# A gated attention and a token mixer in one kernel: the opening planned like the body, transfers handed over later, keys and queries turned as one

## The chip, the cores and the metric

The kernel runs on one core of a Trainium2 chip. The core has a matrix engine (TensorE, PE in the profile), three elementwise engines (VectorE or DVE, ScalarE or ACT, GpSimd or POOL) and SyncE (SP), whose queue only issues transfers here. All transfers run on sixteen DMA engines; some of them turn (transpose) a tile of two-byte numbers on the way. The metric is the device time of one execution in microseconds, lower is better. The kernel before takes 846.6 us, the median of three runs (846.22, 846.6 and 854.43).

## What is computed

```python
# batch 8, seq 3200, d_model 256, d_qk = d_hyper = 64
scores = (1/S) * z @ z.T                  # per batch, 3200 x 3200, symmetric
attn   = maximum(scores, 0) ** 2
x      = u * (attn @ v)                   # 3200 x 256
wq, wk = x @ w_q, x @ w_k                 # 3200 x 64
W_tok  = (1/8) * wq @ wk.T                # 3200 x 3200, no activation
mixed  = W_tok @ x
out    = maximum(mixed, 0) @ w_out        # float32
```

## The kernel before

**Tiles.** The 3200 rows of a batch are 25 tiles of 128. They are also seven groups of columns: six of 512 (four tiles) and one of 128. For each group the kernel goes over all 25 tiles. A score pair (line 220) makes two tiles of `scores` against the group, 128 x 512 each, into one of two PSUM slots. A first stage (lines 239 and 243, ACT or DVE) takes the positive part to SBUF as float32, which empties the slot; a second stage (line 256 on ACT, line 258 on POOL) squares it to fp16 in a buffer `at`, of which there are 14. The second product (line 299) multiplies `at` by v into four accumulator banks, two halves of a group by two half-arrays. Scores are symmetric, so a block of tiles that a group makes for one of the next two groups, or for the last, is not computed again: a DMA transpose (line 278) turns it from `at` into `tt` or `ttl`. Such blocks are called turned tiles.

**After a group.** ACT and DVE add the banks (lines 315 and 316), POOL multiplies by u (line 320) and the result x is turned by DMA (line 345) to `xT`. Projections of x give queries and keys together (line 362), ACT writes them out as fp16 `qk` (line 375). Keys are turned by DMA (line 382), two transposes of 64 rows by 256 columns for each full group, and doubled by POOL (line 394); "heads" (line 401) sum keys times x over all rows, 64 x 256 numbers, since the mixer has no activation between its two products. When a batch is through, "mix" (line 429) and the last product (line 452) make its outputs, beside the next batch's groups. The last groups of the last batch have a sequence of their own from line 946 on.

**z.** The score product wants z turned and standing twice, one copy in each half of the partitions. For batch 0 z is loaded in four chunks as float32, cast twice (line 118), turned on TensorE (line 127) and copied from PSUM (line 130). For later batches POOL's queue loads z as fp16 (line 141), DVE copies it twice in a row (line 146), and five DMA transposes turn it (line 152).

**Order of work.** Every engine and every issuing queue does its instructions in the order written. That order is written by a planner in the kernel's Python (lines 512 to 898): it keeps a clock for each of PE, DVE, ACT and POOL, books a weight for each step, and picks the next step of TensorE by these clocks. A transfer for SP is a `move(ready, due, issue, takes, fn, landed)`: it may be handed over when the PE clock passes `ready`, the one with the earliest `due` goes first, SP is booked for `issue`, and the DMA for `takes`; `landed` then tells the planner when the data can be used. So a transfer that stands early in SP's order, but whose data comes late on the chip, holds up all behind it. POOL's queue also issues loads (v and the later z), between its squares. The weights in the planner are the kernel's own numbers, not measurements.

**Opening.** The first eight score pairs, the first eight tiles of the second product, the chunks of z and the loads of v of batch 0 are written out by hand (lines 816 to 842), with tiles in the order 0 to 24; the planner takes over behind them, with made-up ready times for what the opening has begun. v comes in five loads, which stand in POOL's queue between casts and squares. The weights' seven transfers are issued in one go (line 171).

Of the kernel before, what the change touches and what calls it, by code (L numbers as in the profile page):

```python
# [16 lines left out]
def kernel(  # L17
# [74 lines left out]

    ZCH = [(0, 4), (4, 6), (10, 7), (17, 8)]
    ident = consts.tile([P, P], FP16, tag="ident", name="ident")
# [13 lines left out]

    def cast_first(c):
        n0, nn = ZCH[c]  # L110
        casts = [
            (nc.vector.tensor_copy, nc.scalar.copy),
            (nc.scalar.copy, nc.gpsimd.tensor_copy),
            (nc.gpsimd.tensor_copy, nc.vector.tensor_copy),
            (nc.gpsimd.tensor_copy, nc.vector.tensor_copy),
        ][c]
        for half, cast in enumerate(casts):
            cast(out=zd0[:, n0 : n0 + nn, half, :], in_=z32[n0][:])

    def turn_first(c):  # L120
        n0, nn = ZCH[c]
        if c < 2:
            tp = acc_tile(1, c, "ztp", FP16)
        else:
            tp = pps.tile([P, 4 * W], FP16, tag="ps", name="ztp")
        for i in range(nn):
            nc.tensor.transpose(
                tp[:, ts(i, P)], zd0[:, n0 + i, :, :].rearrange("p a k -> p (a k)"), ident
            )
        nc.vector.tensor_copy(out=zT[0][:, ds(n0 * P, nn * P)], in_=tp[:, 0 : nn * P])  # L130

# [10 lines left out]

    def double_z(b):
        zds[b] = pz.tile([P, NT, 2, dqk], FP16, tag="zd", name="zd")
        for half in range(2):
            nc.vector.tensor_copy(out=zds[b][:, :, half, :], in_=zdense[b][:])

# [23 lines left out]
    def load_weights():  # L171
        wo32[0] = px.tile([P, ND, D], FP32, tag="x_sb", name="wo32")
        for r in range(2):
            for w32, w in ((wq32, moe_w_q), (wk32, moe_w_k)):
                nc.sync.dma_start(out=w32[top(r), :, :], in_=w.rearrange("(c p) h -> p c h", p=dh))
        for half in range(2):
            nc.sync.dma_start(
                out=wk2[:, :, half, :], in_=moe_w_k.rearrange("(c p) h -> p c h", p=P)
            )
        nc.sync.dma_start(out=wo32[0][:], in_=moe_w_out.rearrange("(c p) e -> p c e", p=P))  # L180

# [15 lines left out]
    for b in range(B):  # L197
        for gi in range(NG):
            near = [t for t in range(NT) if is_turned(gi, group_of(t))]
            own = [  # L200
                t for t in range(NT) if t not in near and not is_turned(group_of(t), gi)
            ]
            if b == 0 and gi == 0:
                order = sorted(near + own)
            elif len(tiles) % 2:
                order = own[:1] + near + own[1:]
            else:
                order = near + own
            tiles += [(b, gi, t) for t in order]
            ends[b, gi] = len(tiles)  # L210
# [4 lines left out]
    def scores(p):  # L215
        assert len(ztimes) >= 5 * tiles[2 * p + 1][0]
        sc = ps_tile("sc")
# [159 lines left out]
    def turn_keys(b, gi):  # L377
        nn = widths[gi] // P
        ks[b, gi] = pk.tile([P, 4, 2, dh], FP16, tag="kx", name="kx")
        for r in halves(gi):  # L380
            n = min(2, nn - 2 * r)
            nc.sync.dma_start_transpose(
                out=ks[b, gi][:, 2 * r : 2 * r + n, 1 - r, :],
                in_=qks[b, gi][top(1 - r), r, 0 : n * P],
            )

# [135 lines left out]
    pending, later, extras, keyed, kept = [], [], [], [], []  # L522
    keys_at, out_of, turned_at = {}, {}, {}
    produced, stored = [0], []
# [3 lines left out]
    sp_at, dma_at = [0.0], [0.0]  # L528
    LANDS = 4.0

    def at_time(t, fn):
# [36 lines left out]
    def close_slot(t):  # L568
        slots.append(t)

    def use_pair():
        open_slot()
        p = produced[0]
        produced[0] += 1
        sc = scores(p)
        clock[PE] += 0.22
        ready = clock[PE] + FROM_PE
# [6 lines left out]
    def squares():  # L584
        while pending and pending[0][0] <= clock[PE] + 0.3:
# [25 lines left out]
    def use_keys(b, gi):  # L611
# [7 lines left out]
        if prior:  # L619
# [52 lines left out]
    def use_proj(b, gi):  # L672
# [12 lines left out]

        move(done + 0.2, done + 6.0, 0.55, 1.6, stores[0], landed)

# [4 lines left out]
    def batch_begun(b, t):  # L692
        if b + 1 < B:
            t += 10 if b == 0 else 0
            at_time(t + 6, lambda: (load_z(b + 1), push(3.0)))
            at_time(t + 20, lambda: double_z(b + 1))
            for i in range(5):
                move(t + 24 + 6 * i, t + 40 + 6 * i, 1.5, 1.0, lambda i=i: turn_z(b + 1, i))
            for i in range(5):
                at_time(t + 20 + 13 * i, lambda i=i: (load_v(b + 1, 5 * i, 5), push(2.5)))  # L700

    def group_begun(b, gi, t):
        if gi == 0:
            batch_begun(b, t)
        if gi + 1 < NG:
            move(t + 2, t + 6, 0.55, 1.6, lambda: load_u(b, gi + 1))
        elif b + 1 < B:
            move(t + 2, t + 6, 0.55, 1.6, lambda: load_u(b + 1, 0))

    SPARE = 0.5  # L710
    BIAS = 0.2
    GUARD = 12
    LATE = 0.3

    def half_done(b, gi, half):
# [21 lines left out]
    def open_rows():  # L737
# [6 lines left out]
        b, gi, left, fresh = (current[x] for x in ("b", "gi", "left", "fresh"))  # L744
        ready = [t for t in left if row_at.get((b, gi, t), 1e9) <= clock[PE]]
        mine = [t for t in ready if (b, gi, t) in made]
# [33 lines left out]
    def acc_step():  # L780
# [6 lines left out]
        fn()  # L787
        clock[PE] += 0.1093
        used.add(row)
# [4 lines left out]
    def calm(weight):  # L794
# [5 lines left out]
        return max(first, clock[PE] + 0.5) + weight <= shut + LATE  # L800

    def all_used(p):
        return all(x in used for x in tiles[2 * p : 2 * p + 2])

    accumulate = lambda rows_, first=False: [
        fn()
        for half in range(2)
        for ti in rows_
        for fn in second_product(0, 0, half, ti, first and ti == rows_[0], False)
    ]  # L810

    def first_pair(p, on_act):
        for _, turn in second_stage(p, first_stage(p, scores(p), on_act), on_act):
            turn()

# [9 lines left out]
    first_pair(1, False)  # L825
    cast_first(2)
    first_pair(2, True)
    load_first_v(4, 6)
    accumulate([0, 1], first=True)
    turn_first(2)  # L830
    first_pair(3, False)
    accumulate([2, 3])
    first_pair(4, True)
    cast_first(3)
    load_first_v(10, 8)
    first_pair(5, False)
    accumulate([4, 5])
    turn_first(3)
    first_pair(6, True)
    accumulate([6, 7])  # L840
    first_pair(7, False)
    load_first_v(18, 7)
    produced[0] = 8
    groups.pop(0)
    current.update(b=0, gi=0, left=list(range(8, NT)), fresh=False)
    for p in range(8):
        for x in tiles[2 * p : 2 * p + 2]:
            b, gi, ti = x
            row_at[x] = 0.4 * p - 1.0
            if ti < 8:  # L850
                used.add(x)
            if is_turned(gi, group_of(ti)):
                for n in range(4):
                    row_at[b, group_of(ti), n] = 14.0
    at_time(3.0, lambda: load_u(0, 0))
    at_time(9.0, load_weights)
    at_time(20.0, cast_weights)
    group_begun(0, 0, 0.0)

    total = B * sum(NT * (w // P) for w in widths)  # L860
    done_acc = 32
    lead = 140
    turn_about = False
    while groups or work or current["left"]:
# [15 lines left out]
        p = produced[0]  # L880
        able = p < NPAIR and (p < NAT or all_used(p - NAT) and turned_at.get(p - NAT, 0.0) <= now and not out_of.get(p - NAT))
        wanted = able and p * total < (done_acc + lead) * NPAIR
# [131 lines left out]
```

## Time and profile before

| What | us |
|---|---|
| median of three runs | 846.6 |
| the profiled execution, its own time | 841.71 |
| its span, first to last instruction | 839.9 |
| TensorE busy | 780.0 (93%) |
| POOL busy | 613.7 (73%) |
| ACT busy | 577.6 (69%) |
| DVE busy | 479.1 (57%) |

The profile is of one execution, and its rows have times from the start of the span. A row of a group gives line, engine and operation, output and inputs, shapes, count, busy time, mean time of one in ns, and the idle time just before with what ended it. A row of the timeline begins with its start and its length. A matmul's length in a row holds its way through the array, and one starts before the last ends; so the rate is read from many in a row. DMA queue q1 holds what SP issues, q0 what POOL issues.

### The profile page before, as it was taken

The numbers are of one execution on the slowest core, as the hardware profiler recorded it, in microseconds if no ns is written. First come the engines' busy times: TensorE is split into PE (matmuls) and PEld (weight loads), VectorE is DVE, ScalarE is ACT, GpSimd is POOL, SyncE is SP. The second block draws the span as 40 slices with busy tenths as digits, with TensorE's granted clock in tenths as the row PEclk, the third lists the DMA queues.
The fourth block names the chain that finished last, engine by engine and source line by source line (L and its number), as shares of the span: only waits on it lengthen the run. The fifth ranks groups of instructions, "written<-read, shape, count | busy, mean of one in ns | idle before, by whom it ended". The sixth has DMA issues, their size and how long they took to land. (4 is left out here: it accounts for less than half of the span.)

```text
span 839.9 us, 28273 instructions
## 1 busy us (share of the span) xinstructions
PE 780.0 (93%) x12373; PEld 651.2 (78%) x12373; DVE 479.1 (57%) x501; ACT 577.6 (69%) x672; POOL 613.7 (73%) x513
## 2 busy tenths in 40 slices
PE   5799899999989998889989999999999999999995
PEld 3689788887778887768878877878778878878783
DVE  3576456654576536546558645655546654575533
ACT  4677677775767766756766766777677675877735
POOL 4797577877778657949968666978598886886750
PEclk9999999999999999999999999999999999999999
DMA  5999999999989988999597998999989999888725
GB/s 108 171 189 151 150 164 156 142 193 198 175 155 153 171 192 172 114 225 195 118 166 144 149 207 175 156 155 197 175 177 174 151 197 198 141 149 170 159 59 197
DMA packets 299101, 138.36 MB, mean 165 GB/s; under 512 B 276832, under 2 KB 279776, under 8 KB 298976
## 3 DMA queue, kind: packets, MB, share of 16 engines
q1 hardware_dynamic: 292064, 120.37, 77.5%
q0 software_dynamic: 6768, 15.98, 14.0%
q8 instruction: 97, 1.59, 0.8%
q14 instruction: 28, 0.23, 0.1%
q10 hardware_dynamic: 144, 0.20, 0.1%
HBM read 59.64 MB, written 26.21 MB: 102 GB/s over the span
## 5 line engine op out<-in xcount | busy, mean ns | idle before, releaser
L299 PE MATMUL acc<-v_sb,at 64*128 64x256 f16 x7312 | 500.5, 271 | 9.8 <-DMA v_sb<-in_v_dram 5.0
L258 POOL TENSOR_TENSOR at<-g 128x1024 f16<-128x1024 f32 (+2 forms) x236 | 426.6, 1823 | 80.3 <-DVE g L243 62.6
L299 PEld LDWEIGHTS <-at 64*128 64x128 f16 x7312 | 387.3, 95 | 79.2 <-issue 19.6
L243 DVE TENSOR_SCALAR g<-sc 128x1024 f32<-128x1024 f32 (+2 forms) x302 | 350.5, 1181 | 136.7 <-PE sc L220 123.5
L256 ACT ACTIVATE at<-g 128x1024 f16<-128x1024 f32 (+1 forms) x232 | 243.0, 1052 | 30.5 <-DVE g L243 26.6
L239 ACT ACTIVATE g<-sc 128x1024 f32<-128x1024 f32 x166 | 170.0, 1024 | 79.0 <-PE sc L220 77.9
L220 PE MATMUL sc<-zT 64*128 64x512 f16 x920 | 176.9, 380 | 13.1 <-DVE g L243 11.2
L320 POOL TENSOR_TENSOR x_sb<-both,u_sb 128x512 f16<-128x512 f32 (+1 forms) x112 | 133.0, 1195 | 71.6 <-DVE both L316 68.8
L299 PE MATMUL acc<-v_sb,tt 64*128 64x256 f16 x2304 | 164.1, 269 | 0.0
L316 DVE TENSOR_TENSOR both<-acc,both 128x512 f32<-128x512 f32 (+1 forms) x104 | 69.2, 670 | 129.1 <-ACT both L315 122.2
L299 PEld LDWEIGHTS <-tt 64*128 64x128 f16 x2304 | 121.6, 94 | 13.3
L315 ACT COPY both<-acc 128x512 f32<-128x512 f32 (+1 forms) x104 | 57.9, 563 | 39.7 <-PE acc L299 36.7
L220 PEld LDWEIGHTS <-zT 64*128 64x128 f16 x920 | 55.4, 94 | 28.3 <-issue 20.7
L375 ACT CAST qk<-qk 128x512 f16<-128x512 f32 (+1 forms) x54 | 29.4, 544 | 57.4 <-PE qk L401 52.2
L477 ACT ACTIVATE fo<-fo 128x1024 f32<-128x1024 f32 (+2 forms) x54 | 47.7, 890 | 29.7 <-PE fo L452 22.7
L442 ACT ACTIVATE rt<-mx 128x1024 f16<-128x1024 f32 (+1 forms) x56 | 52.2, 932 | 17.2 <-PE mx L429 17.1
L394 POOL COPY kx<-kx 128x128 f16<-128x128 f16 (+1 forms) x101 | 26.5, 289 | 48.4 <-DMA kx<-qk 48.3
L452 PE MATMUL fo<-wo,rt 128*128 128x256 f16 x400 | 52.8, 274 | 1.8 <-ACT rt L442 1.8
L416 DVE TENSOR_TENSOR ha<-qk,ha 128x512 f32<-128x512 f32 x37 | 25.6, 691 | 47.1 <-ACT qk L375 47.1
L362 PE MATMUL qk<-xT_sb,wqk 64*128 64x256 f16 (+1 forms) x404 | 32.9, 271 | 17.1 <-DMA xT_sb<-x_sb 17.0
L452 PEld LDWEIGHTS <-rt 128*128 128x128 f16 x400 | 35.0, 98 | 16.0 <-issue 10.1
L362 PEld LDWEIGHTS <-wqk 64*128 64x128 f16 x416 | 21.5, 95 | 23.2 <-DMA xT_sb<-x_sb 18.9
(42 smaller groups left out, 220.8 us busy)
## 6 DMA issues: line engine op xcount, KB each, us to landing
u_sb<-in_u_dram SPq DMA_DIRECT2D x48, 512.0 KB, 4.6
out_dram<-fo SPq DMA_DIRECT2D x40, 512.0 KB, 4.9
v_sb<-in_v_dram POOLq DMA_DIRECT2D x35, 320.0 KB, 6.5
out_dram<-fo SPq DMA_DIRECT2D x16, 256.0 KB, 2.0
zn<-in_z_dram POOLq DMA_DIRECT2D x7, 400.0 KB, 7.1
tt<-at SPq DMA_TRANSPOSE x144, 4.5
kx<-qk SPq DMA_TRANSPOSE x101, 3.7
u_sb<-in_u_dram SPq DMA_DIRECT2D x8, 128.0 KB, 3.8
```

Of the source, the lines that this page charges most:

```text
L220: nc.tensor.matmul(out=sc[:, h, 0:gw], lhsT=zT[b][top(h), ts(ti, P)], rhs=zT[b][top(h), ds(gs, gw)], start=True, stop=True,)
L239: nc.scalar.activation(out=g[:, hs, 0:w], in_=sc[:, hs, 0:w], func=RELU, scale=GSCALE)
L243: nc.vector.tensor_scalar(out=g[:, hs, 0:w], in0=sc[:, hs, 0:w], scalar1=0.0, scalar2=GSCALE, op0=AOP.max, op1=AOP.mult,)
L256: nc.scalar.square(out=out, in_=g[:, hs, 0:w])
L258: nc.gpsimd.tensor_mul(out=out, in0=g[:, hs, 0:w], in1=g[:, hs, 0:w])
L299: nc.tensor.matmul(out=accs[half, r][:, ds((j % 2) * D, D)], lhsT=weights(b, gi, ti, j)[top(r), :], rhs=vs[b][top(r), ti, :], start=(first ...
L315: nc.scalar.copy(out=both[:, 0 : n * D], in_=accs[half, 0][:, 0 : n * D])
L316: nc.vector.tensor_add(out=both[:, 0 : n * D], in0=accs[half, 1][:, 0 : n * D], in1=both[:, 0 : n * D])
L320: nc.gpsimd.tensor_mul(out=xs[b, gi][:, 0:n, :, r, :].rearrange("p n c d -> p (n c) d"), in0=both[:, 0 : n * D].rearrange("p (m d) -> p m ...
L362: nc.tensor.matmul(out=ps[:, r, 0 : n * P], lhsT=wqk[top(r), c, :, :].rearrange("p t h -> p (t h)"), rhs=xTs[b, gi][top(r), 0:n, c, :], st ...
L442: nc.scalar.activation(out=out, in_=ps[:, 0:nr, 0 : ND * n * P], func=RELU)
L452: nc.tensor.matmul(out=banks[r][:, ds(j * D, D)], lhsT=flat[:, ds((dc * n + j) * P, P)], rhs=wo[:, dc, :], start=(dc == 0 and j == 0), sto ...
```

## The change

The opening is left to the planner. Tiles of the first group are taken in another order: first those that are not to be turned (0 to 3 and 12 to 23), then 4 to 11 and 24. The chunks of z are loaded and turned in that order, all turns of z stand ahead of the first second product, and go through the four accumulator banks; the copy out of PSUM goes to ACT or DVE by their clocks. All five loads of v are issued on POOL's queue ahead of the first square. The planner's clocks start at times written by hand, PE's weights are doubled before 11 us, and v has times from which it may be used. The loads of u and of the weights become moves.

The planner's model of transfers is changed: SP is booked 1.28 us for each transpose, whatever its size, and 0.21 us of DMA for each 128 columns; SP is held when the DMA is more than 2 us behind (`RING`); a transfer may be handed over 1 us after its data is planned to be there (`SLACK`), not 0.2 or 0.3; x is due for turning 5 us after (`XDUE`), not 8; the projections are planned 3 us after x has landed (`XWAIT`). A load of u is handed over only when POOL's clock has passed.

The two copies of z on DVE are planned 3 us apart and booked with 0.98 us each. Keys and queries of a group are turned by one DMA transpose of 128 rows; the half that holds queries is overwritten by POOL's doubling copy.

```diff
-    ZCH = [(0, 4), (4, 6), (10, 7), (17, 8)]
+    ZCH = [(0, 4), (12, 6), (18, 7), (4, 8)]
...
     def turn_first(c):
...
-        if c < 2:
-            tp = acc_tile(1, c, "ztp", FP16)
-        else:
-            tp = pps.tile([P, 4 * W], FP16, tag="ps", name="ztp")
+        tp = acc_tile(1 - c // 2, c % 2, "ztp", FP16)
...
-        nc.vector.tensor_copy(out=zT[0][:, ds(n0 * P, nn * P)], in_=tp[:, 0 : nn * P])
+        clock[PE] += 0.14 * nn
+        ready = clock[PE] + FROM_PE
+        on_act = max(clock[ACT], ready) < max(clock[DVE], ready)
+        copy = nc.scalar.copy if on_act else nc.vector.tensor_copy
+        copy(out=zT[0][:, ds(n0 * P, nn * P)], in_=tp[:, 0 : nn * P])
+        z_at[c] = give(ACT if on_act else DVE, ready, 0.2 + 0.065 * nn)
...
-    def double_z(b):
-        zds[b] = pz.tile([P, NT, 2, dqk], FP16, tag="zd", name="zd")
-        for half in range(2):
-            nc.vector.tensor_copy(out=zds[b][:, :, half, :], in_=zdense[b][:])
+    def double_z(b, half):
+        if half == 0:
+            zds[b] = pz.tile([P, NT, 2, dqk], FP16, tag="zd", name="zd")
+        nc.vector.tensor_copy(out=zds[b][:, :, half, :], in_=zdense[b][:])
...
+        for i, (t, w) in enumerate(loads):
+            move(18.0 + i, 26.0 + i, 0.65, 0.5, lambda t=t, w=w: nc.sync.dma_start(out=t, in_=w))
...
             if b == 0 and gi == 0:
-                order = sorted(near + own)
+                order = own + near
...
     def turn_keys(b, gi):
         nn = widths[gi] // P
         ks[b, gi] = pk.tile([P, 4, 2, dh], FP16, tag="kx", name="kx")
-        for r in halves(gi):
-            n = min(2, nn - 2 * r)
-            nc.sync.dma_start_transpose(
-                out=ks[b, gi][:, 2 * r : 2 * r + n, 1 - r, :],
-                in_=qks[b, gi][top(1 - r), r, 0 : n * P],
-            )
+        nc.sync.dma_start_transpose(
+            out=ks[b, gi][:, 0:nn, :, :].rearrange("p n a h -> p n (a h)"),
+            in_=qks[b, gi][:].rearrange("p r s -> p (r s)")[:, 0 : nn * P],
+        )
...
     LANDS = 4.0
+    RING = 2.0
+    SLACK = 1.0
...
         begun = max(sp_at[0], clock[PE])
-        sp_at[0] = begun + issue
         dma_at[0] = max(dma_at[0], begun) + takes
+        sp_at[0] = max(begun + issue, dma_at[0] - RING)
...
+    def cold():
+        return 2.0 if clock[PE] < 11.0 else 1.0
...
-                move(done + 0.3, due, 0.31 * n, 0.2 * n, turn, lambda t, x=(p, b, gi, gj, nn): block_landed(t, *x))
+                move(done + SLACK, due + SLACK, 1.28, 0.21 * n, turn, lambda t, x=(p, b, gi, gj, nn): block_landed(t, *x))
...
-            done + 0.3, done + 10.0, 0.17 * n, 0.1 * n, lambda: turn_keys(b, gi),
+            done + SLACK, done + 10.0, 1.28, 0.21 * n, lambda: turn_keys(b, gi),
...
-            t += 10 if b == 0 else 0
+            t += 6 if b == 0 else 0
             at_time(t + 6, lambda: (load_z(b + 1), push(3.0)))
-            at_time(t + 20, lambda: double_z(b + 1))
+            for half in range(2):
+                at_time(
+                    t + 18 + 3 * half,
+                    lambda half=half: (double_z(b + 1, half), give(DVE, clock[PE], 0.98)),
+                )
             for i in range(5):
-                move(t + 24 + 6 * i, t + 40 + 6 * i, 1.5, 1.0, lambda i=i: turn_z(b + 1, i))
+                move(t + 24 + 6 * i, t + 40 + 6 * i, 1.28, 1.05, lambda i=i: turn_z(b + 1, i))
...
-            move(t + 2, t + 6, 0.55, 1.6, lambda: load_u(b, gi + 1))
+            move(max(t + 2, clock[POOL] + SLACK), t + 7, 0.55, 1.6, lambda: load_u(b, gi + 1))
...
+    XDUE = 5.0
+    XWAIT = 3.0
...
-                t + 0.3, t + 8.0, 0.31 * n / 2, 0.2 * n / 2, lambda: turn_x(b, gi),
+                t + SLACK, t + XDUE, 1.28, 0.21 * n, lambda: turn_x(b, gi),
...
-            add_extra(t, "keys", lambda: use_keys(b, gi))
+            add_extra(t + XWAIT, "keys", lambda: use_keys(b, gi))
...
-            if not take or (fresh and len(take) < 6):
+            if not take or (fresh and len(take) < (6 if b or gi else 2)):
...
     make_identity(nc, ident)
     load_first_z()
     load_first_v(0, 2)
     cast_first(0)
-    turn_first(0)
     cast_first(1)
     load_first_v(2, 2)
-    first_pair(0, True)
-    turn_first(1)
...
+    cast_first(2)
+    load_first_v(12, 6)
+    cast_first(3, [0])
+    load_first_v(18, 7)
+    load_first_v(4, 8)
+    clock[:] = [4.5, 4.95, 4.7, 7.8]
+    v_at = [4.5] * 2 + [8.2] * 2 + [18.7] * 8 + [11.2] * 6 + [14.7] * 7
+    dma_at[0] = 16.0
+    turn_first(0)
+    cast_first(3, [1])
+    give(DVE, 0.0, 0.65)
+    turn_first(1)
+    current.update(b=0, gi=0, left=list(range(NT)), fresh=True)
+    groups.pop(0)
+    use_pair()
+    use_pair()
     turn_first(2)
...
     turn_first(3)
...
+    move(10.0, 14.0, 0.55, 1.6, lambda: load_u(0, 0))
+    load_weights()
+    at_time(38.0, cast_weights)
+    group_begun(0, 0, 12.0)
```

More of the change, by code (lines that the diff above doesn't have):

```diff
@@ L215, in scores @@
     def scores(p):
-        assert len(ztimes) >= 5 * tiles[2 * p + 1][0]
+        assert len(ztimes) >= 5 * tiles[2 * p + 1][0] and p_chunk(p) in z_at, (p, clock, len(ztimes), z_at)
         sc = ps_tile("sc")
@@ L705, in group_begun @@
         if gi + 1 < NG:
[L706 removed]
+            move(max(t + 2, clock[POOL] + SLACK), t + 7, 0.55, 1.6, lambda: load_u(b, gi + 1))
         elif b + 1 < B:
[L708 removed]
+            move(max(t + 2, clock[POOL] + SLACK), t + 7, 0.55, 1.6, lambda: load_u(b + 1, 0))
     SPARE = 0.5
@@ L745, in open_rows @@
         ready = [t for t in left if row_at.get((b, gi, t), 1e9) <= clock[PE]]
+        if b == 0 and gi == 0:
+            ready = [t for t in ready if v_at[t] <= clock[PE]]
         mine = [t for t in ready if (b, gi, t) in made]
@@ L800, in calm, with p_chunk @@
         return max(first, clock[PE] + 0.5) + weight <= shut + LATE
+    def p_chunk(p):
+        t = [x[2] for x in tiles[2 * p : 2 * p + 2]]
+        return max(c for c, (n0, nn) in enumerate(ZCH) for i in t if n0 <= i < n0 + nn) if p < 12 else 3
     def all_used(p):
         return all(x in used for x in tiles[2 * p : 2 * p + 2])
[L805 to L814, printed above, removed]
     make_identity(nc, ident)
@@ L880 @@
         p = produced[0]
-        able = p < NPAIR and (p < NAT or all_used(p - NAT) and turned_at.get(p - NAT, 0.0) <= now and not out_of.get(p - NAT))
+        able = p < NPAIR and z_at[p_chunk(p)] <= now and (p < NAT or all_used(p - NAT) and turned_at.get(p - NAT, 0.0) <= now and not out_of.get(p - NAT))
         wanted = able and p * total < (done_acc + lead) * NPAIR
```

55 lines of the change are left out of this document (11 added, 44 removed).

## The prediction

> **What bounds the kernel now.** I read the page's first line, then the busy time of the opening and the body, then who makes TensorE wait.
>
> ```profile
> span 839.9 us, 28273 instructions
> ```
>
> ```profile
> 0.00:40.00 40.00, 26.88 (x306) 18.87 (x308) 17.56 (x20) 22.30 (x24) 24.59 (x25) 0.96 0.75 141
> 40.00:815.00 775.00, 738.51 (x11947) 623.08 (x11942) 453.43 (x468) 542.54 (x630) 587.72 (x486) 1.00 0.95 165
> ```
>
> The columns of a stretch are its length, then busy us and count of PE, PEld, DVE, ACT and POOL, the granted clock, the DMA share and GB/s. TensorE is the bound: 738.5 of 775 us in the body, while no elementwise engine passes 76% there (587.7/775). So time can only be won where TensorE stands still or runs slowly: 13 us in the first 40 and 36 in the body. The tail behind 815 us (written from line 900 on) isn't edited. Who it waits for in the body, and two rows of the chain of waits that give the dense rate:
>
> ```profile
> PE qk L362 <- DMA xT_sb<-x_sb: 17.0, 10, 4.1
> PE sc L220 <- DVE g L243: 10.2, 12, 1.7
> ```
>
> ```profile
> 731.22 0.43 PE sc L220 x4
> 731.65 2.95 PE acc L299 x54
> ```
>
> Two causes hold 27 of the 36 us: ten waits for the turned x ahead of the projections (17.0 us), and twelve of a score pair for a PSUM slot that DVE has not emptied (10.2). A dense second-product matmul takes 2.95/54 = 0.0546 us, a score 0.43/4 = 0.108. With these I price the opening's work.
>
> ```profile
> L299 PE MATMUL acc<-v_sb,at 64*128 64x256 f16 x239 | 19.3, 305 | 6.0 <-DMA v_sb<-in_v_dram 5.0 <-DVE both L316 0.5 <-ACT both L315 0.4
> L220 PE MATMUL sc<-zT 64*128 64x512 f16 x42 | 9.5, 461 | 1.6 <-DVE g L243 1.0 <-DVE zT L130 0.5
> L127 PE MATMUL ztp<-ident,zd 128*128 128x128 f16 x25 | 3.0, 278 | 5.5 <-DVE zd L118 4.5 <-POOL zd L118 1.0
> ```
>
> These are the groups of TensorE's first 40 us. At the dense rate they are 239 x 0.0546 + 42 x 0.108 + 25 x 0.055 = 13.0 + 4.5 + 1.4 = 19 us of work. The opening loses 21 us, more than its idle time shows, because much of it ran slowly.
>
> **The opening (order of z, v, turns and squares).**
>
> ```profile
> 11.17 0.59 POOL L107 DMA_DIRECT2D v_sb<-in_v_dram  x1
> ```
>
> ```profile
> 12.54 1.92 PE L299 MATMUL acc<-v_sb,at 64*128 64x256 f16 x16
> 14.24 1.04 PE L220 MATMUL sc<-zT 64*128 64x512 f16 x4
> 17.06 1.05 PE L299 MATMUL acc<-v_sb,at 64*128 64x256 f16 x16 [1.78 <-DMA v_sb<-in_v_dram]
> ...
> 36.22 1.05 ACT L315 COPY both<-acc 128x512 f32<-128x512 f32 x2
> ```
>
> The three late v loads (the first is shown) stand in POOL's queue behind squares; TensorE waits 5.0 us for them, and the first group closes at 36.2, when ACT takes its sums. In the new order POOL issues them right behind its casts of z (0.5 to 0.6 us each), by my estimate at about 5.3, 6.5 and 7.1 us. Here is what they take, and what the elementwise steps take:
>
> ```profile
> v_sb<-in_v_dram POOLq DMA_DIRECT2D x1, 512.0 KB, 8.0
> v_sb<-in_v_dram POOLq DMA_DIRECT2D x1, 448.0 KB, 7.5
> v_sb<-in_v_dram POOLq DMA_DIRECT2D x1, 384.0 KB, 5.8
> ```
>
> ```profile
> L258 POOL TENSOR_TENSOR at<-g 128x1024 f16<-128x1024 f32 (+2 forms) x236 | 426.6, 1823 | 80.3 <-DVE g L243 62.6
> ```
>
> ```profile
> L243 DVE TENSOR_SCALAR g<-sc 128x1024 f32<-128x1024 f32 (+2 forms) x302 | 350.5, 1181 | 136.7 <-PE sc L220 123.5
> L256 ACT ACTIVATE at<-g 128x1024 f16<-128x1024 f32 (+1 forms) x232 | 243.0, 1052 | 30.5 <-DVE g L243 26.6
> ```
>
> Alone they would land at 5.3 + 5.8 = 11, 6.5 + 7.5 = 14 and 7.1 + 8.0 = 15 us; sharing the engines, the last may reach 19. The three elementwise engines together make 1/1.05 + 1/1.18 + 1/1.82 = 2.35 steps per us; a pair of tiles needs two, so a pair every 0.85 us. TensorE needs 2 x 8 x 0.0546 + 0.22 = 1.1 us a pair, so it is the bound again once squares flow. The first product now starts at 8.4; I put it at 9, since a wait is added: all four accumulator banks hold turned z first, and their copies (0.4 to 0.7 us each on ACT and DVE) stand among the first score copies. Behind that wait stand only the products themselves. Up to 18 us the 16 tiles 0 to 3 and 12 to 23 have their v, 16 x 8 x 0.0546 = 7 us of second product and 3 of scores; the turned tiles 4 to 11 come last, when their v is in. So the new loss by 40 us is 9 - 1.8 = 7.2 before the first product, 2 for the half rate until about 13 (it lasts to about 15 now, with breaks that go), 2 for thin production, 1 for the close of the group: 12 to 13 instead of 21. I take **8 us won**; bounds 5 (half rate to 16, v last at 19) and 11 (dense from 9). The turned tiles land later, but nothing waits for any turned tile now:
>
> ```profile
> L299 PE MATMUL acc<-v_sb,tt 64*128 64x256 f16 x2304 | 164.1, 269 | 0.0
> ```
>
> At 12.5 us sixteen products took 1.92 us, at 17.1 only 1.05, and four scores at 14.2 took 1.04 instead of 0.43: half rate up to about 15, which the granted clock of that stretch (0.96) doesn't tell. The Trainium skill, "TensorE: Matmul & The Clock Gate", Part 4, says that transposes in transpose mode do not count as activity for the clock gate. If so, the 25 turns put first wake nothing, the half rate runs to about 15 as it does now, and the opening wins 7 rather than 8; the trace cannot separate this, since turns and products are mixed in it.
>
> **The turned x (lines 345 and 362; handing to SP, due time 5, three us of delay).**
>
> ```profile
> 348.98 6.74 SPq L278 DMA_TRANSPOSE tt<-at  x2
> 349.57 1.29 POOL L320 TENSOR_TENSOR x_sb<-both,u_sb 128x512 f16<-128x512 f32 x1
> ...
> 362.51 2.65 SPq L345 DMA_TRANSPOSE xT_sb<-x_sb  x1
> ...
> 367.22 1.03 PE L362 MATMUL qk<-xT_sb,wqk 64*128 64x256 f16 x8 [4.10 <-DMA xT_sb<-x_sb]
> ```
>
> This is the longest of the ten. x is ready at 350.9, but SP takes it at 362.5, behind transposes of tiles, the first two of which held SP for 6.7 us; it lands at 367.2 and TensorE has stood for 4.1. The edits answer it twice: x is due 5 rather than 8 us after it is ready, so fewer transposes pass it, and the projections are planned 3 us later, with products ahead of them. A shift by 3 us alone leaves 4.1 - 3 = 1.1 of this wait and nothing of the others, if none other was over 3 (17.0 over ten has a mean of 1.7). Handing over at 1.0 instead of 0.3 us takes 0.7 back. I take **14 of 17.0**; bounds 5 (the queue grows as much as the margin) and 17.
>
> A wait is followed by slow work:
>
> ```profile
> 367.00:370.00 3.00, 2.78 (x26) 1.85 (x28) 0.23 (x1) 0.85 (x2) 0.00 (x0) 0.50 1.05 294
> 435.00:438.40 3.40, 2.96 (x28) 1.97 (x30) 0.41 (x1) 1.03 (x2) 0.68 (x1) 0.50 1.63 210
> 435.44 1.03 PE L362 MATMUL qk<-xT_sb,wqk 64*128 64x256 f16 x8 [2.53 <-DMA xT_sb<-x_sb]
> ```
>
> After the two longest waits the granted clock is 0.50 for 3.4 us, 1.7 us lost each: **3 us more won** (0 to 3.4). The same page of the Trainium skill ("Why this matters for your kernels") warns only of idle gaps above about 3 us; by that the 2.53 us wait would cost nothing and the sum would be 1.7, but the trace shows 0.50 after it too.
>
> **Copies of z apart (line 146).**
>
> ```profile
> 56.07 1.87 DVE L146 COPY zd<-zn 128x1600 f16<-128x1600 f16 x2
> ...
> 59.12 0.39 PE L220 MATMUL sc<-zT 64*128 64x512 f16 x2 [0.71 <-DVE g L243]
> ...
> 644.82 0.39 PE L220 MATMUL sc<-zT 64*128 64x512 f16 x2 [0.75 <-DVE g L243]
> ```
>
> Both halves run back to back, 1.87 us that the plan does not book on DVE; a score pair then waits for its slot. These are the first copies with the wait behind them, and the last of seven such waits; the waits three us behind the seven copies are 7.6 of the 10.2 us. Split by 3 us and booked (0.98 each), one copy is less than the slack of one step: **5 us won**, bounds 0 (same DVE work, wait only divided) and 7.6.
>
> **Keys and queries turned as one.**
>
> ```profile
> L278 SPq DMA_TRANSPOSE ttl<-at x48: 1200/1217/2542, 40.5 to 792.6; - x48
> ```
>
> ```profile
> L382 SPq DMA_TRANSPOSE kx<-qk x101: 1130/1227/2621, 66.0 to 809.8; - x101
> ```
>
> ```profile
> q1 hardware_dynamic: 292064, 120.37, 77.5%
> ```
>
> The first two rows give min/median/max of an issue in ns, the third packets, MB and share of a queue. Of the 101 issues 47 go (one instead of two for each full group): 47 x 1.23 = 58 us of SP's queue, worth nothing by itself but it lets transfers behind pass. The new transpose has the shape of ttl (128 rows x 512 columns), 1.22 us of issue. Its rows double: 2 x 2 x 64 more 256-byte rows per full group, 47 x 256 + 7 x 64 = 12,480 packets. At q1's mean, 0.775 x 839.9 x 16 / 292064 = 0.0357 us, that is 12,480 x 0.0357 / 16 = 28 us of all sixteen engines over the span. POOL's doubling copies remain as they are. The body's DMA share of 0.95 is no ceiling, since the 435 row shows 1.63, so I take 2 us lost (0 to 28, nearer to the first).
>
> **Rest.** u is handed to SP only when POOL is done with its old buffer. No row shows TensorE or POOL waiting for u, so it costs nothing while u is early by more than the gate. Weights keep their seven DMAs and five POOL casts, spread over the first 38 us; the first keys, which need them, are turned at 66 us (the L382 row), so there is cover of some 20 us. Work buffers (14) stay held 0.7 us longer; new waits of this kind I put at 1 us (0 to 6, the size of the present small ones).
>
> **Sum.** - 8 - 14 - 3 - 5 + 2 + 1 = -27 us on the profiled 841.7 (span 839.9 and 1.8 around it), so 815. The median of the three runs, 846.6, stands 4.9 above that execution; the same difference gives 846.6 - 27 = **820 us**.
>
> **Rivals.** *All waits named go*: 11 + 17 + 3.4 + 7.6 = 39, so 808. For it: every one has a cause that an edit addresses. Against: a new order moves buffers, and something is late next. *Only the opening and the copies*: the later hand-over eats the margin, x still arrives as projections start; 8 + 5 = 13, so 834. For it: the x wait is a backlog of DMA, and nothing reduces the bytes. *No effect*: the order that the planner writes makes as many waits elsewhere as it removes; 846. *DMA becomes the bound*: the doubled rows land on the chain, 28 us, and with the turned tiles late the 17 us of x stay; 846.6 - 8 - 5 + 28 = 862. It decides once the DMA engines cannot rise above their present 0.95 in the body, so that most of the 28 us is added; against it stand stretches above 1.0.
>
> **Numbers.** Forecast (812 to 828) 0.45; full gain (under 812) 0.17; opening and copies (828 to 838) 0.18; no effect (838 to 855) 0.10; DMA bound (over 855) 0.10. About 1%, 8 us, is what a measurement here can tell from no change: faster 0.80, same 0.10, slower 0.10. The range leaves out the best of the full gain and the slow end: 804 to 850.
>
> **What would show it.** First group closed at 24 to 27 us instead of 36, no v wait above 1 us; waits for xT under 4 us in all; waits for g under 6; no granted clock of 0.50 between 40 and 815; 54 key transposes, about 304,500 packets on q1. Wrong if TensorE starts to wait for turned tiles or for squares, or if the DMA share rises while SP's issues stretch.

## The result and the profile after

The changed kernel takes 799.1 us (four executions, 798.8 to 801.1), the kernel before, run beside it, 848.6 (846.2 to 854.4): the ratio is 0.941, 95% interval 0.936 to 0.947. The forecast was 820 with a range of 804 to 850; the sign was right, the size was not, and the time lies under the range. The profiled execution took 799.1 us, so between the two profiled executions the change is 841.7 - 799.1 = 42.6 us.

The busy time of the changed kernel in the opening, in the body and in the tail (columns as in the prediction):

```profile
span 797.3 us, 28226 instructions
...
0.00:40.00 40.00, 33.13 (x458) 27.49 (x460) 24.07 (x25) 26.50 (x28) 31.37 (x31) 1.00 0.86 166
40.00:772.00 732.00, 723.60 (x11801) 625.31 (x11796) 443.66 (x455) 531.84 (x624) 603.18 (x489) 1.00 0.96 178
772.00:797.30 25.30, 15.36 (x123) 9.04 (x120) 7.98 (x14) 12.28 (x20) 0.52 (x2) 0.87 0.49 182
...
core 0: 797.3 us, clock 0.996
```

TensorE stands still for 732.0 - 723.6 = 8.4 us of the body, where it was 36.5 before. The mean granted clock of 0.996 (last row), in which the half rate of the opening doesn't show, means some 3 us lost in the whole span, and the tail, 25.3 us at 0.87, holds all of it: no stretch of half rate is left in the body. TensorE's longest waits in the body:

```profile
PE sc L223 <- DVE g L246: 4.3, 6, 1.0
PE acc L302 <- DVE both L319: 1.4, 3, 0.5
PE mx L430 <- DVE ha L417: 1.4, 2, 1.0
```

No wait for turned x (17.0 us before, now line 365) is left in the body. The group that had the longest wait in the kernel before (group 1 of batch 3), in the changed kernel's timeline:

```profile
326.28 2.50 POOL L323 TENSOR_TENSOR x_sb<-both,u_sb 128x512 f16<-128x512 f32 x2
...
330.94 1.25 SPq L348 DMA_TRANSPOSE xT_sb<-x_sb  x1
...
344.65 0.60 PE L365 MATMUL qk<-xT_sb,wqk 64*128 64x256 f16 x8
```

x is ready at 328.8, SP takes it 2.2 us later (11.7 before), and the projections come 13.7 us behind that, without a wait. The groups of TensorE in the first 40 us:

```profile
L302 PE MATMUL acc<-v_sb,at 64*128 64x256 f16 x351 | 25.2, 282 | 1.5 <-DMA v_sb<-in_v_dram 1.0 <-DVE both L319 0.5
L223 PE MATMUL sc<-zT 64*128 64x512 f16 x50 | 11.3, 439 | 0.1
L125 PE MATMUL ztp<-ident,zd 128*128 128x128 f16 x25 | 3.2, 309 | 5.2 <-DVE zd L119 4.6 <-POOL zd L119 0.6
L302 PE MATMUL acc<-v_sb,tt 64*128 64x256 f16 x32 | 2.7, 269 | 0.0
```

At the dense rates of the prediction that is 383 x 0.0546 + 50 x 0.108 + 1.4 = 27.7 us of work instead of 19: the opening now loses 12.3 us instead of 21. So of the 42.6 us some 9 are the opening's, and 34 the body's: 28 us of idle time, 3.4 for the two stretches of half rate, and some 2 us that these rows don't place.

### The profile page after: what moved, and what is told of

The parts are those of the page before. It is cut to its first block, busy times and chain, and to the rows that moved or that the text cites. A ratio compares the mean times of both kernels' runs of the same rounds, so it can differ in the third digit from the quotient of the medians.

```text
span 797.3 us, 28226 instructions
## 1 busy us (share of the span) xinstructions
PE 772.1 (97%) x12373; PEld 661.8 (83%) x12373; DVE 475.7 (60%) x494; ACT 570.6 (72%) x671; POOL 635.1 (80%) x521
## 3 DMA queue, kind: packets, MB, share of 16 engines
q1 hardware_dynamic: 303040, 123.55, 78.6%
## 4 chain that ended last, share of the span: by engine, by line
PE 90%; DVE 4%; DMA 2%; issue 1%; ACT 1%; POOL 1%; SPq 0%; DVEq 0%; ACTq 0%
PE acc L302 66%; PE sc L223 12%; PE fo L453 6%; PE qk L365 3%; PE qk L402 2%; DVE g L246 2%; PE mx L430 1%; DMA v_sb<-in_v_dram 1%; DVE ha L417 1%; DVE hs L424 1%; DMA out_dram<-fo 1%; DVE both L319 1%; POOL x_sb L323 0%; DMA z<-in_z_dram 0%; ACT both L318 0%
## 5 line engine op out<-in xcount | busy, mean ns | idle before, releaser
L261 POOL TENSOR_TENSOR at<-g 128x1024 f16<-128x1024 f32 (+2 forms) x244 | 448.6, 1853 | 70.2 <-DVE g L246 60.7
L302 PEld LDWEIGHTS <-at 64*128 64x128 f16 x7312 | 397.1, 94 | 61.8 <-issue 9.7
L246 DVE TENSOR_SCALAR g<-sc 128x1024 f32<-128x1024 f32 (+1 forms) x296 | 345.1, 1186 | 133.7 <-PE sc L223 121.9
L259 ACT ACTIVATE at<-g 128x1024 f16<-128x1024 f32 (+1 forms) x224 | 230.6, 1036 | 23.3 <-DVE g L246 19.4
L242 ACT ACTIVATE g<-sc 128x1024 f32<-128x1024 f32 x172 | 174.9, 1018 | 68.6 <-PE sc L223 67.8
L223 PE MATMUL sc<-zT 64*128 64x512 f16 x920 | 180.1, 379 | 5.1 <-DVE g L246 4.3
L302 PEld LDWEIGHTS <-tt 64*128 64x128 f16 x2304 | 125.4, 94 | 11.6 <-issue 0.4
L223 PEld LDWEIGHTS <-zT 64*128 64x128 f16 x920 | 58.6, 94 | 19.1 <-issue 14.6
L402 PE MATMUL qk<-x_sb,kx 64*128 64x256 f16 x354 | 29.0, 269 | 0.0
```

The costliest lines, as they stand in the source:

```text
L223: nc.tensor.matmul(out=sc[:, h, 0:gw], lhsT=zT[b][top(h), ts(ti, P)], rhs=zT[b][top(h), ds(gs, gw)], start=True, stop=True,)
L242: nc.scalar.activation(out=g[:, hs, 0:w], in_=sc[:, hs, 0:w], func=RELU, scale=GSCALE)
L246: nc.vector.tensor_scalar(out=g[:, hs, 0:w], in0=sc[:, hs, 0:w], scalar1=0.0, scalar2=GSCALE, op0=AOP.max, op1=AOP.mult,)
L259: nc.scalar.square(out=out, in_=g[:, hs, 0:w])
L261: nc.gpsimd.tensor_mul(out=out, in0=g[:, hs, 0:w], in1=g[:, hs, 0:w])
L302: nc.tensor.matmul(out=accs[half, r][:, ds((j % 2) * D, D)], lhsT=weights(b, gi, ti, j)[top(r), :], rhs=vs[b][top(r), ti, :], start=(first ...
```

## The experiments

Theory A said that each part of the change removes the wait that it was aimed at, and nothing new comes in its place; its rivals stand in the expectations. The experiments either undo a part in the changed kernel or do a part alone in the kernel before. Those of one set ran beside the kernel before, whose median was 844.7 us in the first set, 838.6 in the second, 842.0 in the third and 846.7 in the last; "beside" means this median. The changed kernel itself was not run again in these sets, so a difference from its 799.1 us is one between sets; its four executions lie within 2.4 us, and most of the kernels below were run four times.

### The opening and the body apart

`opening_only` keeps the old model and constants, the copies together and two key transposes in the changed kernel; `body_only` puts the changed model and constants, the copies apart and the single key transpose into the kernel before:

```diff
# opening_only, from the changed kernel
-    RING = 2.0
-    SLACK = 1.0
+    RING = 1e9
+    SLACK = 0.3
-    XDUE = 5.0
-    XWAIT = 3.0
+    XDUE = 8.0
+    XWAIT = 0.0
...
# body_only, from the kernel before: the changed lines of the body, and
-            t += 10 if b == 0 else 0
+            t += 4 if b == 0 else 0
-                move(t + 24 + 6 * i, t + 40 + 6 * i, 1.5, 1.0, lambda i=i: turn_z(b + 1, i))
+                move(t + 24 + 6 * i, t + (40 if b else 32) + 6 * i, 1.28, 1.05, lambda i=i: turn_z(b + 1, i))
```

> The changed opening alone; the planner's model of transfers, the hand-over times, the due and wait of x, the copies of z and the key transposes are as before. If the waits are additive (theory A: each part removes the waits it was aimed at and nothing new comes in their place), the loss of the opening goes from 21 to 13 us and the body keeps its 17 us of waits for turned x: about 8 us under the kernel before, 838 to 842. If the body's gain comes out of the new opening as well, because the order that the planner writes behind it differs (theory B), it is under 825.

> Everything but the opening, on the hand-written opening of before; batch 1's z is begun 4 instead of 6 us later and due 8 us earlier, so that it is turned in time behind the shorter planned first batch. Theory A: the 8 us of the opening are missing and nothing else, 806 to 812. Theory B: over 825.

Measured: `opening_only` 840.0 us, ratio 0.996 (0.990 to 1.002); `body_only` 806.1, ratio 0.961 (0.954 to 0.968). So the body's gain doesn't come out of the opening's order (theory B falls), and the opening is worth some 7 us when the body is in place (806.1 against 799.1). Without it, the opening's 4.7 us are not clear of the scatter. The first 40 us of `opening_only` and its wait for x, in a profiled execution of 844.4 us:

```profile
0.00:40.00 40.00, 33.39 (x454) 27.31 (x456) 24.76 (x26) 25.47 (x27) 28.98 (x28) 1.00 0.84 156
...
PE qk L365 <- DMA xT_sb<-x_sb: 25.9, 15, 4.2
```

The opening is as full as in the changed kernel (454 instructions of TensorE against 458). The wait for x was 25.9 us there, against 17.0 in the profile of the kernel before. That may be why less of the opening's gain shows, but it is one execution, 4 us above the median, and this was not tested.

### The shift of the projections and the model of transfers

> The changed kernel with x due 8 us after it is ready instead of 5 and the projections planned when x has landed instead of 3 us later. Theory A1 (the shift is what removes the wait): TensorE waits for turned x again, 12 to 17 us in all, and the time is 812 to 818. Theory A2 (the truer model of SP and of the DMA removes it, the shift is only a margin on top): waits under 5 us, 800 to 805. The margins between landing and projection, 4 to 12 us in the changed kernel, fall by about 3 under either.

> The changed kernel with the old bookings of transfers (SP booked by the size of a transpose, no hold by the DMA's backlog), the old hand-over 0.3 us after the data, and u handed over by time alone; the shift of the projections, the due time 5, the copies of z apart and the keys turned as one stay. Theory A1: the shift still covers the lag of SP, 800 to 806. Theory A2: turned x comes late again by more than 3 us in the places where SP lags by 10 us or more, and the time is over 812.

Measured: `no_xwait` 804.9 us (798.7 to 815.2), `old_model` 803.7 (800.5 to 804.7). Either can go for some 5 us, and for `no_xwait` even that is rough, since its executions lie 16 us apart; neither theory A1 nor A2 gave both. Neither profile has a wait of TensorE for x, but that of `no_xwait` is its best execution, 798.7 us. What `old_model` waits for instead is one store:

```profile
PE qk L365 <- ACT fo L478: 5.4, 1, 5.4
...
557.32 1.02 ACT L478 ACTIVATE fo<-fo 128x1024 f32<-128x1024 f32 x1 [7.87 <-DMA out_dram<-fo]
```

The turned x of that group had landed at 551.2, 5.6 us after its issue. ACT stood 7.9 us for a store of the output, issued at 548.8, which took 8.4 us to land (the median of these is under 5), and the projections stood behind ACT. So in this execution what `old_model` loses is not a wait for x. Then both were undone together:

> The changed kernel with both undone together: the old bookings and hand-over of transfers, and x due 8 us after it is ready with no shift of the projections. The copies of z apart, the keys turned as one and the opening stay. Either alone cost 5 us or less. Theory C (two covers for one wait: the shift covers SP's lag, the truer model takes the lag away, and one of them is enough): here the waits for turned x are back, 15 us or more, and the time is 818 to 835. Theory D (what remains, the single key transpose and the copies apart, took the lag away): waits for x under 6 us, 800 to 808.

Measured: 820.6 us (816.6 to 825.7), 21.5 above the changed kernel where the two alone cost 5.8 and 4.6. TensorE's waits in the body of `no_both`:

```profile
PE qk L365 <- DMA xT_sb<-x_sb: 18.0, 9, 5.0
PE sc L223 <- DVE g L246: 4.5, 6, 1.1
```

Theory C holds: two covers for one wait. The wait for x is back in its old size, 18.0 us, and of the three profiles only in the one without both. And the opening, the copies apart and the single key transpose, which stayed, are together still worth some 18 us beside the kernel before.

### The shift alone, the copies alone, the keys alone

```diff
# before_shift
-                t + 0.3, t + 8.0, 0.31 * n / 2, 0.2 * n / 2, lambda: turn_x(b, gi),
+                t + 0.3, t + 5.0, 0.31 * n / 2, 0.2 * n / 2, lambda: turn_x(b, gi),
-            add_extra(t, "keys", lambda: use_keys(b, gi))
+            add_extra(t + 3.0, "keys", lambda: use_keys(b, gi))
# before_keys: turn_keys as in the change, the old bookings
# before_z: double_z and its two times as in the change
# z_together, from the changed kernel
+            at_time(t + 18, lambda: (double_z(b + 1, 0), double_z(b + 1, 1)))
```

> The kernel before with x due 5 us after it is ready and the projections planned 3 us later; nothing else. If the shift is a cover of its own (theory C), the waits for turned x fall from 17 us to under 4, the granted clock of 0.50 in the body goes, and the time is 17 to 20 us under the kernel before, some 822 to 828. If the shift needs the single key transpose or the truer model to work, less than 10 us.

> The kernel before with one key transpose of 128 rows for each full group, with the old bookings; nothing else. Putting the two transposes back into the changed kernel cost 10.7 us, with 8 us of waits for x. If SP's queue is what makes x late (theory S), 58 us less of issues takes 5 to 12 us here; if the 12,480 added rows are felt as well, less or nothing.

> The kernel before with the copies of z 3 us apart and booked on DVE; nothing else. The waits of score pairs for DVE were 10.2 us, 7.6 of them behind the copies; putting the copies together in the changed kernel cost 4 us. 3 to 7 us under the kernel before.

> The changed kernel with both copies of z back to back on DVE and not booked, at the time of the first half. Waits of score pairs for DVE's first stage rise by the 5 to 7.6 us that the prediction gave this part: 804 to 807. If the plan has slack there now, nothing: 798 to 801.

| Kernel | us | ratio to before, 95% |
|---|---|---|
| before_shift | 828.9 | 0.985 (0.980 to 0.990) |
| before_keys | 822.6 | 0.979 (0.973 to 0.985) |
| before_z | 834.2 | 0.990 (0.986 to 0.994) |
| z_together | 803.3 | 4.2 us above the changed kernel |

The single key transpose, which the prediction booked as a loss of 2 us, is the largest part: 19 us alone, more than the 5 to 12 that were expected by then. TensorE's waits in the body, first of `before_keys` (in its best execution, 817.7 us), then of `before_shift`:

```profile
PE sc L220 <- DVE g L243: 10.3, 12, 1.7
PE qk L362 <- DMA xT_sb<-x_sb: 2.5, 2, 1.4
```

```profile
PE sc L220 <- DVE g L243: 7.8, 11, 1.4
PE qk L362 <- DMA xT_sb<-x_sb: 7.8, 2, 5.8
PE acc L299 <- POOL at L258: 3.0, 2, 2.3
```

With the keys in one transpose and nothing else, the wait for x falls from 17.0 to 2.5 us, more than with the shift that was made for it (7.8, in two waits, one of 5.8, which a shift of 3 doesn't cover). The shifted order also has 3.0 us of waits for squares, which were 0.4. The wait for DVE, 10.2 before, stays in `before_keys`; the copies apart take care of it, 8 us alone. TensorE's wait for DVE in the body of `before_z` (whose profiled execution took 842.0 us and waited 23.6 us for x), and in that of `z_together`:

```profile
PE sc L220 <- DVE g L243: 1.7, 2, 0.9
...
PE sc L223 <- DVE g L246: 3.5, 8, 1.0
```

With the copies put together again in the changed kernel this wait does not come back (3.5 us against 4.3), although the expectation was built on it. The 4.2 us of `z_together` (799.6 to 805.2) have no shown cause.

### Why the key transposes cost

The single transpose has 47 issues fewer and 12,480 rows more. `keys_two` puts two transposes of 64 rows for each full group back into the changed kernel, `keys_split` two of 128 rows, with every engine's order written as in `keys_two`; `before_split` widens the two of the kernel before. `keys_two_wait6` gives `keys_two` a longer shift.

```diff
# keys_split, from keys_two
-                out=ks[b, gi][:, 2 * r : 2 * r + n, 1 - r, :],
-                in_=qks[b, gi][top(1 - r), r, 0 : n * P],
+                out=ks[b, gi][:, 2 * r : 2 * r + n, :, :].rearrange("p n a h -> p n (a h)"),
+                in_=qks[b, gi][:, r, 0 : n * P],
# keys_two_wait6, from keys_two
-    XWAIT = 3.0
+    XWAIT = 6.0
```

> The changed kernel with two key transposes of 64 rows for each full group again, booked as two issues. If the queue of SP matters (58 us more of issues), the time rises by 3 us or more; if the 28 us of DMA that the single transpose adds cost anything, it falls by up to that. I expect neither: 797 to 803.

> The changed kernel with two key transposes for each full group, each of all 128 rows and 256 columns: as many issues as in keys_two and every engine's order the same as there, but the bytes of the single transpose. Theory S1 (the number of issues in SP's queue is what costs): as keys_two, 806 to 813. Theory S2 (a transpose of 64 rows is what is slow, in the DMA): as the changed kernel, 798 to 802. If the added bytes cost as well, over 813.

> The kernel before with its two key transposes widened to 128 rows and nothing else: the same order and number of issues as before, and the 12,480 added rows. Theory S1: nothing is won, 838 to 848, and if the rows are felt up to 28 us more. Theory S2: most of the 19 us of before_keys, 822 to 828.

> The changed kernel with two key transposes again and the projections planned 6 instead of 3 us after x has landed. If the 10.7 us of the two transposes come only through x that lands too late (theory S), the longer shift covers it: waits for x under 2 us, 799 to 803. If SP's longer queue makes something else late (turned tiles, keys), it stays at 806 or more.

Measured: `keys_two` 809.8 us (805.6 to 814.3), `keys_split` 811.6 (807.0 to 816.0), `before_split` 850.3, ratio 1.005 (1.000 to 1.010). The number of issues is what matters, not the shape (theory S1): two issues cost the changed kernel 11 to 12 us whatever their width, which `keys_two` was not expected to do, and the width alone wins nothing on the kernel before. The added rows, which the prediction bounded by 28 us, cost 2 us between `keys_two` and `keys_split`, within their scatter, and 4 between `before_split` and before, about its uncertainty. The waits for x of TensorE and for turned keys of POOL, in the kernel before, in `before_split` and in `before_keys`:

```profile
PE qk L362 <- DMA xT_sb<-x_sb: 17.0, 10, 4.1
POOL kx L394 <- DMA kx<-qk: 48.3, 14, 7.7
...
PE qk L362 <- DMA xT_sb<-x_sb: 20.6, 12, 3.6
POOL kx L394 <- DMA kx<-qk: 47.2, 17, 5.9
...
PE qk L362 <- DMA xT_sb<-x_sb: 2.5, 2, 1.4
POOL kx L392 <- DMA kx<-qk: 12.6, 5, 4.4
```

Both waits stay with two wide transposes and fall with one. So fewer issues bring the keys earlier too, and POOL, which stood 48 us for them before its doubling copies, stands 13. For the group of the longest wait the lag in SP's queue can be seen directly in `before_keys`:

```profile
341.84 1.29 POOL L320 TENSOR_TENSOR x_sb<-both,u_sb 128x512 f16<-128x512 f32 x1
...
349.56 1.31 SPq L345 DMA_TRANSPOSE xT_sb<-x_sb  x1
```

x is ready at 343.1 and SP takes it 6.4 us later, where it was 11.7. How much of the 19 us comes through x and how much through the keys was not separated. The queue and the wait in `keys_split`:

```profile
q1 hardware_dynamic: 304544, 123.56, 80.5%
...
PE qk L365 <- DMA xT_sb<-x_sb: 7.7, 3, 5.3
```

and the same in `keys_two`:

```profile
q1 hardware_dynamic: 292064, 120.37, 77.2%
...
PE qk L365 <- DMA xT_sb<-x_sb: 8.3, 4, 3.6
```

The packets differ by 12,480, as worked out, and the wait for x by 0.6 us. `keys_two_wait6` took 809.1 us in all four executions (808.9 to 809.4). Its wait for x is gone and so is its scatter, but no time is won, which I had not expected: the 10 us above the changed kernel aren't x. From 774 us on the heads wait for keys, and the last product for ACT; the third row gives the granted clock:

```profile
PE hd L404 <- POOL kx L397: 3.9, 3, 2.0
PE fo L455 <- ACT rt L445: 2.6, 3, 1.7
...
core 0: 807.2 us, clock 0.990
```

The changed kernel has no such wait of the heads. TensorE stands still for 30.1 us of this span and for 25.2 of the changed kernel's, and 3.9 of the 4.9 us more are the heads. Its busy time is 777.1 us against 772.1, with the same instructions; the granted clock, 0.990 of 807.2 us against 0.996 of 797.3, is 5 us more lost to half rate, which is this difference. One such stretch follows two waits of 1.1 and 1.2 us near 55 us; the others stand in the tail, the first behind the waits of the heads.

### The half rate in the opening

```diff
# warm_products, ahead of the first turn of z
+    idle = ps_tile("idle")
+    for i in range(30):
+        nc.tensor.matmul(out=idle[:, 0, ts(i % 4, P)], lhsT=ident, rhs=ident, start=True, stop=True)
```

> The changed kernel with 30 products of the identity on TensorE ahead of the first turn of z, while z is under way; their result is not used. If the half rate up to 15.7 us is the gate's answer to TensorE's idle start and to turns that do not count, full rate comes by about 8 us and the time falls by 2 to 4 us, to 795 to 797. If the opening is held by squares and by v and not by the rate, nothing changes: 798 to 800.

Measured: 800.9 us (798.9 to 805.3), nothing won. TensorE's timeline there:

```profile
1.37 3.38 PE L839 MATMUL idle<-ident 128*128 128x128 f16 x30 [1.37 <-POOL ident masks.py:199]
...
6.72 0.56 PE L125 MATMUL ztp<-ident,zd 128*128 128x128 f16 x7
...
9.14 0.61 PE L223 MATMUL sc<-zT 64*128 64x512 f16 x4
10.93 1.04 PE L302 MATMUL acc<-v_sb,at 64*128 64x256 f16 x8 [1.18 <-DMA v_sb<-in_v_dram]
...
12.80 2.58 PE L302 MATMUL acc<-v_sb,at 64*128 64x256 f16 x22
```

The products did bring the full rate, early: seven turns in 0.56 us, where the changed kernel takes 0.93. But TensorE then waits 1.2 us for the last chunk of z and 1.2 us for v, and from 10.9 us it is at half rate again, until about 17. In this execution the rate was lost at the waits, not missing for want of a start.

## Why the prediction was wrong

**The opening: the sum right, its parts not.** First product at 9, close at 24 to 27, loss 12 to 13: it was 11.3, 27.5 and 12.3. The first product came 2.3 us late and the half rate held to about 15.7 instead of 13; the other terms of the loss must have been smaller by as much, so that the sum came out is in part luck. The first product waits 1.0 us for the second load of v:

```profile
2.15 0.91 SPq L163 DMA_DIRECT2D u_sb<-in_u_dram  x2
3.10 0.43 SPq L183 DMA_DIRECT2D wo<-in_moe_w_out_dram  x1
4.28 0.53 POOL L107 DMA_DIRECT2D v_sb<-in_v_dram  x1
...
11.31 1.04 PE L302 MATMUL acc<-v_sb,at 64*128 64x256 f16 x8 [1.01 <-DMA v_sb<-in_v_dram]
```

That load landed 6.9 us after its issue; in the kernel before the same load, issued at 4.1, took 2.9. New beside it are the loads of u and the first weight: as moves they stand ahead of the first turned tile in SP's order, and since SP has nothing to wait for there, u is issued at 2.2 us, not at the planned 10; the kernel before issues it at 24.6. In all ten profiles with u at 2.1 or 2.2 us this load of v took 6.1 to 6.9 us, in all six with u at 24.6 or later 2.9 to 3.7. The prediction priced the move of u at nothing. If that is the cause, it is about 3 us of that load; no run changed u alone. The last chunk of z landed later too, 5.6 us after its issue against 3.3 (4.5 to 4.9 in the other profiles with the old opening), which set POOL back: the last two loads of v were issued at 8.2 and 8.7 us instead of 6.5 and 7.1. 8 us taken, about 9 found in the loss and 7 in the time of `body_only`.

**Keys as one: wrong, in sign.** This is the step that failed: the 47 issues were put as "58 us of SP's queue, worth nothing by itself but it lets transfers behind pass", with nothing in the sum for the passing, and with 2 us lost to DMA. The runs showed 19 us won alone and 11 when undone, and the runs with two wide transposes showed that it is the issues, not the shape. The prediction had the fact in its hands: x stood 11.7 us in SP's queue behind other transfers, and 47 of the issues in that queue went. I booked the queue's relief as if SP had time to spare, although the longest wait was a wait in that queue. The added rows did cost DMA time as worked out (see the last section), but hardly any of it became the kernel's. The forecast of 304,500 packets on q1 was off by 1,500 (303,040), which is 32 for each of the 47 issues.

**Turned x: the mechanism right, the size too small.** I took 14 of 17.0 and 3 of 3.4: all of both went. It needed no single part: the shift alone leaves 7.8 us and takes 13 us off, the keys alone leave 2.5 and take 19 off, and in the changed kernel the shift or the model may go for some 5 us, both for 21.5. My sum gave the wait to one pair of edits and let the third pass at nothing.

**Copies of z: sized about right.** 5 taken; the wait for DVE fell from 10.2 to 4.3 us, and the time by 8 alone. The 4 us when undone are not this wait, as said above.

**New waits: none of the kind.** The 1 us for buffers held longer, the 2 for DMA and the withheld rests of each term were 39 - 27 = 12 us of caution together. The rival with all waits gone, 808 with 0.17, was the nearest; on the profiled executions it says 841.7 - 39 = 802.7 and the chip 799.1. Term by term, the forecast of 815 for the profiled execution was some 16 us too high: 3 for the two losses that did not come, 3.4 for x and its half rate, 1.6 for the opening and the copies, 5 for waits of the body that the sum did not name (9.3 us before, 4.1 after: for the sums, for turned z, for keys), and some 2 not placed.

**The step from the profile to the median: wrong.** I carried the 4.9 us between the profiled execution and the median over to the changed kernel. The executions of the kernel before lay between 832 and 850 for the most part, with medians from 838.6 to 848.6 from set to set. The profiled one, 841.7, was an ordinary one among them (the middle of the 50 on record is 843.7), and the three behind the 846.6 happened to be longer. Those of the changed kernel lie within 2.4 us and its profiled one at the median. That is 4.9 us of the 21 by which the forecast was high.

**DMA bound, and no effect: did not come.** The body's DMA share is 0.96 against 0.95, and TensorE has no wait for turned tiles.

## What to carry over

When a wait is a wait in a queue, everything that leaves this queue is part of its price: count the issues that go, and don't book them at nothing because they aren't on the chain themselves. When several edits answer one wait, price them as covers for it and not as a sum; undone one by one each looks cheap, and only together do they show. A time at which the planner hands a transfer over is only a place in the order: if the queue is free, the transfer starts at once, as u did at 2.2 us. And the scatter of executions is a reading too: it was 1 to 3% from set to set in the kernel before, 0.3% in the changed kernel, and it went from 8.8 us in `keys_two` to 0.5 in `keys_two_wait6`, where the wait for x went. So a difference between one profiled execution and a median should not be carried over to a kernel without these waits.

## What the runs showed of the hardware

Turning 128 rows instead of 64 cost SP the same 1.2 us of issue (median 1.23 us in `keys_two`, 1.24 in `keys_split`). It cost the DMA engines what the prediction worked out: 12,480 more rows of 256 bytes raised q1's share from 77.2% of 812.6 us to 80.5% of 814.1, which is 28 us of all sixteen engines; the kernel's time rose by 2 us, within the scatter. After two waits of TensorE of 1.2 us each the half rate came back: in `warm_products` full rate was there at 6.7 us and gone at 10.9. The rule of the Trainium skill that turns do not count for the clock gate ("TensorE: Matmul & The Clock Gate", Part 4) isn't borne out here: in `no_both` seventeen turns and four scores were all that TensorE had done when the next turns ran at full rate, eight in 0.62 us.

```profile
4.13 1.30 PE L125 MATMUL ztp<-ident,zd 128*128 128x128 f16 x10 [4.13 <-ACT zd L119]
5.36 1.04 PE L223 MATMUL sc<-zT 64*128 64x512 f16 x4
6.33 0.93 PE L125 MATMUL ztp<-ident,zd 128*128 128x128 f16 x7
8.80 0.62 PE L125 MATMUL ztp<-ident,zd 128*128 128x128 f16 x8 [1.54 <-POOL zd L119]
```

TensorE had worked for about 3.1 us by then, and 2.2 of these were turns. In the changed kernel's own profiled execution the same order of work did not bring the full rate there (eight turns at 8.3 us took 1.03), so the moment differs from execution to execution.
